# Query columns grouped by dimension, one tile fewer in VectorE's exponential, and paired P·V steps merged, in a four-layer attention kernel

## The chip, the cores and the metric

The kernel runs on one core of a Trainium2 chip. A core has five engines that run their own instruction queues: TensorE (PE) multiplies matrices, and its weight loads are shown apart as PEld; VectorE (DVE) and ScalarE (ACT) work element by element; GpSimd (POOL) does a little side work; SyncE (SP) issues the DMAs. Engines wait for one another on semaphores. Matrix products land in PSUM, everything else lives in SBUF or, for what is set aside, in DRAM.

The metric is the device time of one execution in microseconds (us), the median of the runs shown.

## The reference

The input is a sequence of 2048 tokens with 512 features, in float32. Four layers follow one another, with the weights A, B, A, B. Each layer normalizes, makes 32 query heads of 16 dimensions and one shared key and value head (multi-query attention), takes softmax attention over all 2048 tokens without a mask, and adds the projected result to its input:

```python
def layer(x, wq, wk, wv, wo):          # _A_ref and _B_ref are the same function
    q = (x @ wq).reshape(B, S, H, Dh).transpose(0, 2, 1, 3)   # S 2048, H 32, Dh 16
    k = x @ wk
    v = x @ wv
    scores = jnp.einsum("bhqd,bkd->bhqk", q, k) * (Dh ** -0.5)
    p = jax.nn.softmax(scores, axis=-1)
    o = jnp.einsum("bhqk,bkd->bhqd", p, v)
    return o.transpose(0, 2, 1, 3).reshape(B, S, H * Dh) @ wo

x = A_x
x = x + layer(_layernorm(x), A_wq, A_wk, A_wv, A_wo)
x = x + layer(_layernorm(x), B_wq, B_wk, B_wv, B_wo)
x = x + layer(_layernorm(x), A_wq, A_wk, A_wv, A_wo)
x = x + layer(_layernorm(x), B_wq, B_wk, B_wv, B_wo)
```

The exponentials are the bulk of the elementwise work: 4 layers x 32 heads x 2048 x 2048.

## The kernel before, in words

**Tiling of the attention.** The work is cut into 64 pairs `(l, b, m)`: layer, block of 512 queries, and one of four groups of eight heads. For a pair, the keys come in chunks of 64; one chunk is two halves (`halves`), and a half is a score tile of 128 partitions x 1024 elements. `score()` (letter S of the order) writes one half into a PSUM tile `st` with eight small products that TensorE runs side by side (64 rows by 32 columns each, at eight places of the array), and ScalarE takes its exponential into one of the 16 tiles of `pts` (named `pt` in the trace), line 756. There are two `st` tiles, so TensorE can be one half ahead.

**Exponentials on VectorE.** Of the 4096 halves, 374 do not go to ScalarE. `score_v` puts the scores of such a half, 24 halves ahead of the rest, into the PSUM tile `by_v`, 512 columns at a time; `exp_first` (letter I, line 785) scales them to an integer in the int32 tile `e`; and a chain of six instructions (letters 0 and 1) follows: take the mantissa bits into `mant` (line 800), keep the exponent bits in `e` (line 802), and four multiply-adds that build a polynomial in `pt` and multiply it by `e` (line 794). `e` and `mant` exist twice, so two chains can be open.

**P·V.** `pv(odd)` multiplies 256 queries of two finished halves by the values, in float32, and adds to one of two PSUM tiles `acc`, for the even and the odd rows of the array. The letter `a` does both rows at once. A chunk needs two such steps, `n` = 0 and 1, for queries 0 to 255 and 256 to 511. A float32 product is shown in the trace as two passes, each with a weight load. After the four reads of a chunk (two rows, two `n`) its two `pt` tiles are free again.

**Everything else** (layer norm, the products for K, V, Q and the output, all in split float16 pairs) goes through one PSUM tile `beside`: TensorE's steps of it are the letters N and M inside b to q, VectorE's steps the letter X. Queries of a pair: `q_clamp` (line 420) and `q_rest` (line 427) make a high and a low float16 part `qs` of 128 partitions x 512 queries, partition = head x 16 + dimension, and SyncE stores them to the DRAM scratch `qscr` in four transfers (line 430), one for each half of the heads and each part. Later `load_q` (letter Q, line 724) reads the scratch back with the heads side by side into `qt`. `sq` and `lengths` use the query squares with a small matrix of zeros and ones, `bones`.

**Weights.** For each layer `load_w` brings four chunks of 128 rows of `wq` and `wo` into one of two `wst` buffers, `w_hi` (line 325) makes the high float16 part of a chunk and `w_lo` (line 328) the low part; the load of chunk c + 2 follows `w_lo` of chunk c.

**What sets the order.** Before the main loop a scheduler orders the instructions of the start (the first normalization, the first `wq`, the first queries, K and V). From there on the order of all engines is the string `ORDER` of 14,315 letters, read one by one; each letter emits its instructions in program order on their engines. An engine runs its own queue in order, so a letter decides what stands behind what.

```python
if what == "S":
    score()
elif what in STEPS:
    step(what)
```

Of the kernel before, what the change touches and what calls it, by code (L numbers as in the profile page):

```python
# [201 lines left out]
         "p": "M-", "q": "-M", "r": "V-", "s": "-V"}  # L202


class Work:


# [25 lines left out]
def fast_path(ctx, tc, x_in, weights, out, flag):  # L233
# [79 lines left out]
    def load_w(key, c):  # L313
# [2 lines left out]
        SP.dma_start(t, w[c * P:(c + 1) * P, :])  # L316
        stat[key, c] = t

    def begin_w(key):
        wt[key] = [one.tile([P, NC, D], F16, name=f"{key[0]}{k}") for k in range(2)]  # L320

    def w_hi(key, c):
        if c == 0:
            begin_w(key)
        V.tensor_scalar(wt[key][0][:, c], stat[key, c], WS, None, ALU.mult)

    def w_lo(key, c):
        V.scalar_tensor_tensor(wt[key][1][:, c], stat.pop((key, c)), WS, wt[key][0][:, c],
                               ALU.mult, ALU.subtract)

    def range_w(i, key):
        n = NL * NB + 4 * i + 2 * (key == "wo")
# [92 lines left out]
    def q_rest(l, b, m, ps):  # L425
        qs = stat.pop(("qs", l, b, m))
        V.tensor_tensor(qs[:, 1], ps, qs[:, 0], ALU.subtract)
        for h in range(2):
            for t in range(2):
                SP.dma_start(qscr[l % 2][b][m][h, t].rearrange("d h q -> h d q"),  # L430
                             qs[64 * h:64 * h + 64, t])
        done.add(("q", l, b, m))

    def lengths(l, b, ps):
# [343 lines left out]
    def exp_first():  # L778
        r, new = pend.popleft()
        if new is not None:  # L780
            k = now["e"] = 1 - now["e"]
            assert len(chains) < 2
            fresh.append((one.tile([P, 1024], I32, name=f"e{k}"), k, new))
        e, k, n = fresh[-1]
        V.tensor_scalar(e[:, 512 * r:512 * r + 512], by_v, SCALE / UP / UP * LOG2E * 2.0 ** 23, LEAD,  # L785
                        ALU.mult, ALU.add)
        if new is not None:
            return
        i = tile_of[n]
        p = pts[:, i]  # L790
        mant = one.tile([P, 1024], F32, name=f"mant{k}")

        def write(k, a, c, b):
            n = V.scalar_tensor_tensor(p, a, c, b, ALU.add, ALU.mult).ins  # L794
            if k == 0 and writer[i] is not None:
                tc.declare_no_dep(n, writer[i], reason="behind the reads in between")
            writer[i] = n

        chains.append(deque([
            lambda: V.tensor_scalar(mant.bitcast(I32), e, 0x7FFFFF, 0x3F800000, ALU.bitwise_and,  # L800
                                    ALU.bitwise_or),
            lambda: V.tensor_scalar(e, e, 0x7F800000, None, ALU.bitwise_and),  # L802
            lambda: write(0, mant, C3, mant),
            lambda: write(1, p, C2, mant),
            lambda: write(2, p, C1, mant),
            lambda: write(3, p, C0, e.bitcast(F32))]))

    def chain(k):
        chains[k].popleft()()
        if not chains[k]:  # L810
            chains.pop(k)

    def pv(odd):
        g, c, n = parts[odd].popleft()
        pr, c0, c1 = groups[g]
# [6 lines left out]
        cs = slice(256 * n, 256 * n + 256)  # L822
        x = [pts[:, i[j % 2], (j // 2) * 512 + 256 * n:(j // 2) * 512 + 256 * n + 256]
             for j in range(4)]
        seen.extend(unit)
        read[g, c] = read.get((g, c), 0) + 1
        if read[g, c] == 4:
            ended.extend(unit)
        last = (c, n) == (2 * c1 - 1, 1)
# [6 lines left out]
    def step(what):  # L836
        ops = [[], []]
        for r, w in enumerate(STEPS[what]):
            if w in "EO":
                assert r == "EO".index(w)  # L840
                ops[r].append(pv(r))
            if w in "VW":
                ops[r].append(score_v(r))
            for _ in range({"N": 2, "M": 1, "W": 1}.get(w, 0)):
                ops[r].append(work.next_pe().step(r))
        both(ops)
        for u in seen:
            sees(u)
        seen.clear()
        for u in ended:  # L850
            free.append(tile_of.pop(u))
        ended.clear()
        for g, odd in ends:
            group[odd] += 1
            add_sums(g, odd)
        ends.clear()
# [143 lines left out]

    plan()
    with tc.manual_schedule():
        for what in ORDER:
# [181 lines left out]
```

## Time and profile before

| | |
|---|---|
| median of the runs | 3551.18 us |
| runs | 3549.01, 3551.18, 3562.09 us |
| the profiled execution: time | 3529.43 us |
| its span, first to last instruction | 3527.6 us |
| mean granted TensorE clock | 0.994 |
| busy: PE / DVE / ACT / POOL | 3424.3 / 3288.6 / 3429.4 / 158.8 us |
| exponentials on ScalarE / on VectorE | 3722 / 374 |

The profile is of one execution, which was 21.75 us faster than the median of the timed runs. A group's row gives the engine, the operation, the tiles written and read, the count, then busy time and mean duration, and last the idle time of the engine before these instructions with what ended most of it. Consecutive instructions of an engine overlap at their ends, so a mean duration can be longer than the distance from one start to the next. In a row of the timeline the first two numbers are the start and the duration, both in us, and a bracket gives idle time before it.

### The profile page before, as it was taken

The numbers are of one execution on the slowest core, as the hardware profiler recorded it, in microseconds if no ns is written. First come the engines' busy times: TensorE is split into PE (matmuls) and PEld (weight loads), VectorE is DVE, ScalarE is ACT, GpSimd is POOL, SyncE is SP. The second block draws the span as 40 slices with busy tenths as digits, with TensorE's granted clock in tenths as the row PEclk, the third lists the DMA queues.
The fourth block names the chain that finished last, engine by engine and source line by source line (L and its number), as shares of the span: only waits on it lengthen the run. The fifth ranks groups of instructions, "written<-read, shape, count | busy, mean of one in ns | idle before, by whom it ended". The sixth has DMA issues, their size and how long they took to land.

```text
span 3527.6 us, 234143 instructions
## 1 busy us (share of the span) xinstructions
PE 3424.3 (97%) x111859; PEld 2162.8 (61%) x111859; DVE 3288.6 (93%) x4417; ACT 3429.4 (97%) x3728; POOL 158.8 (5%) x110
## 2 busy tenths in 40 slices
PE   7999999999999999999999999999999999999997
PEld 4666666665666666666566666665656666665653
DVE  4869999999989999999998999999999999999994
ACT  6999999999999999999999999999999999999996
POOL 1000001000000000000000010000000010000000
PEclk9999999999999999999999999999999999999999
DMA  2121111111012111011111111101101111111110
GB/s 93 64 74 45 43 42 33 32 40 46 27 43 63 32 43 48 27 49 36 31 31 60 48 45 50 33 31 39 50 23 37 54 43 35 45 34 40 32 33 20
DMA packets 91837, 149.56 MB, mean 42 GB/s; under 512 B 28985, under 2 KB 45369, under 8 KB 90873
## 3 DMA queue, kind: packets, MB, share of 16 engines
q1 hardware_dynamic: 90872, 134.49, 12.0%
q8 instruction: 876, 14.35, 1.6%
q14 instruction: 89, 0.72, 0.1%
HBM read 90.57 MB, written 34.59 MB: 35 GB/s over the span
## 4 chain that ended last, share of the span: by engine, by line
PE 44%; ACT 43%; DVE 11%; DMA 1%; issue 1%; SPq 0%; POOL 0%; DVEq 0%; ACTq 0%; POOLq 0%
ACT pt L756 43%; PE acc L475 23%; PE st L475 12%; PE beside L475 6%; DVE pt L794 5%; DVE e L785 1%; PE by_v L475 1%; DVE mant L800 1%; DVE e L802 1%; PE beside L372 1%; PE beside L512 1%; DMA rec<-rs 0%; DVE sum L877 0%; SPq L913 0%; DMA qt<-qs 0%
## 5 line engine op out<-in xcount | busy, mean ns | idle before, releaser
L756 ACT ACTIVATE pt<-st 128x1024 f32<-128x1024 f32 x3722 | 3425.2, 1118 | 46.0 <-PE st L475 41.2
L475 PE MATMUL acc<-pt,vop 64*32 64x256 f32 x65536 | 2830.9, 377 | 6.1 <-issue 3.7
L475 PE MATMUL st<-qt,kop 64*32 64x512 f16 x29776 | 1654.3, 381 | 55.1 <-ACT pt L756 36.4
L475 PEld LDWEIGHTS acc<-pt,vop 64*32 64x32 f32 x65536 | 1460.8, 106 | 364.7 <-issue 19.3
L475 PEld LDWEIGHTS <-kop 64*32 64x32 f16 x32768 | 771.3, 90 | 806.2 <-issue 514.8
L794 DVE SCALAR_TENSOR_TENSOR pt<-pt,mant 128x1024 f32<-128x1024 f32 x748 | 913.5, 1221 | 3.7
L785 DVE TENSOR_SCALAR e<-by_v 128x512 int32<-128x512 f32 x748 | 514.0, 687 | 61.2 <-PE by_v L475 33.6
L794 DVE SCALAR_TENSOR_TENSOR pt<-pt,e 128x1024 f32<-128x1024 f32 x374 | 458.6, 1226 | 0.8
L475 PE MATMUL beside<-xnT,wq 64*32 64x512 f16 x5952 | 456.8, 376 | 2.0 <-DVE gv L415 1.1
L794 DVE SCALAR_TENSOR_TENSOR pt<-mant 128x1024 f32<-128x1024 f32 x374 | 455.4, 1218 | 0.0
L475 PE MATMUL beside<-wo,ot 64*32 64x512 f16 x5664 | 432.1, 376 | 4.7 <-issue 2.4
L475 PE MATMUL by_v<-qt,kop 64*32 64x512 f16 x2992 | 298.7, 377 | 2.9 <-DVE e L785 1.5
L802 DVE TENSOR_SCALAR e<-e 128x1024 int32<-128x1024 int32 x374 | 256.7, 686 | 3.2
L800 DVE TENSOR_SCALAR mant<-e 128x1024 int32<-128x1024 int32 x374 | 257.4, 688 | 1.0
L475 PEld LDWEIGHTS <-wq 64*32 64x32 f16 x5952 | 172.4, 92 | 49.3 <-issue 7.9
L475 PEld LDWEIGHTS <-ot 64*32 64x32 f16 x5664 | 163.9, 92 | 49.8 <-issue 10.3
L423 POOL TENSOR_TENSOR sq<-qs 128x512 bf16<-128x512 f16 x64 | 107.9, 1686 | 1066.6 <-DVE qs L420 1066.6
L877 DVE COPY sum<-acc 128x512 f32<-128x512 f32 x128 | 84.4, 682 | 39.4 <-PE acc L475 39.0
L475 PE MATMUL beside<-xnT,wkv 64*32 64x512 f16 x1440 | 107.7, 376 | 0.0
L359 POOL TENSOR_TENSOR rstd<-var,nhalf 128x4 f32<-128x4 f32 x16 | 25.9, 1621 | 1126.5 <-DVE var L358 1126.5
L420 DVE TENSOR_SCALAR qs<-beside 128x512 f16<-128x512 f32 x63 | 43.1, 684 | 25.8 <-PE beside L475 13.3
L448 DVE SCALAR_TENSOR_TENSOR xt<-beside,xt 128x512 f32<-128x512 f32 x64 | 43.8, 684 | 12.3 <-PE beside L512 11.1
(105 smaller groups left out, 755.2 us busy)
## 6 DMA issues: line engine op xcount, KB each, us to landing
qt<-qs SPq DMA_DIRECT2D x85, 512.0 KB
qs<-qs SPq DMA_DIRECT2D x256, 64.0 KB
rec<-rs SPq DMA_DIRECT2D x63, 256.0 KB
xs<-xt SPq DMA_DIRECT2D x48, 256.0 KB
xt<-xs SPq DMA_DIRECT2D x48, 256.0 KB
xt<-in_A_x_dram SPq DMA_DIRECT2D x32, 256.0 KB
sum<-sum SPq DMA_DIRECT2D x252, 32.0 KB
out_dram<-xt SPq DMA_DIRECT2D x16, 256.0 KB
```

Of the source, the lines that this page charges most:

```text
L372: PE.transpose(ps[:, c * P:(c + 1) * P], xn[:, c * P:(c + 1) * P], ident)
L420: V.tensor_scalar(qs[:, 0], ps, BIG, -BIG, ALU.min, ALU.max)
L423: G.tensor_tensor(sq, qs[:, 0], qs[:, 0], ALU.mult)
L448: V.scalar_tensor_tensor(x, ps, 1 / VS / WS, x, ALU.mult, ALU.add)
L475: PE.matmul(o[32 * j:32 * j + 32], w[j][h], x[j][h], start=start, stop=stop, skip_group_check=True, tile_position=(64 * r, 32 * j))
L512: PE.matmul(beside, w, x, start=n == 0, stop=n == 3 * NC - 1)
L756: e = A.activation(pts[:, i], st[s], AF.Exp, scale=SCALE / UP / UP).ins
L785: V.tensor_scalar(e[:, 512 * r:512 * r + 512], by_v, SCALE / UP / UP * LOG2E * 2.0 ** 23, LEAD, ALU.mult, ALU.add)
L794: n = V.scalar_tensor_tensor(p, a, c, b, ALU.add, ALU.mult).ins
L800: lambda: V.tensor_scalar(mant.bitcast(I32), e, 0x7FFFFF, 0x3F800000, ALU.bitwise_and, ALU.bitwise_or),
L802: lambda: V.tensor_scalar(e, e, 0x7F800000, None, ALU.bitwise_and),
L877: V.tensor_copy(sums[pr, odd], acc[odd])
```

## The change

Three things are changed, and `ORDER` stays letter for letter the same.

1. **Query columns by dimension.** `w_hi` and `w_lo` write the columns of `wq` in another order: within 64 columns, dimension by dimension with four heads side by side, where it was head by head. `w_lo` does it in four instructions of 128 columns. The queries then stand in the partitions in the order in which the scratch holds them, and `q_rest` stores both parts of 64 rows with one transfer, two in all, in place of four whose outermost dimension was 4. `bones` follows the new order. What is stored and what `load_q` reads stays the same.
2. **The integer in the exponential's own tile.** `exp_first` writes its integers straight into the `pt` tile of the half; the tile `e` is gone. The polynomial is built in a new tile `poly` (two of them), and only the last multiply-add writes `pt`.
3. **Merged P·V.** When an `a` with `n` = 0 is followed by another `a` with nothing for TensorE between them, both are done in one step of 512 queries; the second letter is skipped. This happens at 201 places: 1608 products of 512 columns take the place of 3216 of 256, of 32,768.

```diff
@@ prologue
-        V.tensor_reduce(bones[:, 0, 0:8], ident.rearrange("p (a b) -> p a b", b=DH), axis=AX.X,
-                        op=ALU.add)
+        V.tensor_reduce(bones[:, 0, 0:8].rearrange("p (r h) -> p r h", h=4),
+                        ident.rearrange("p (r d h) -> p r h d", d=DH, h=4), axis=AX.X, op=ALU.add)
...
+    def by_heads(key, w):
+        return w.rearrange("p (a h d) -> p a h d", h=4, d=DH) if key[0] == "wq" else w
+
+    def by_dims(key, w):
+
+        return w.rearrange("p (a d h) -> p a h d", h=4, d=DH) if key[0] == "wq" else w
...
-        V.tensor_scalar(wt[key][0][:, c], stat[key, c], WS, None, ALU.mult)
+        V.tensor_scalar(by_dims(key, wt[key][0][:, c]), by_heads(key, stat[key, c]), WS, None, ALU.mult)
 
     def w_lo(key, c):
-        V.scalar_tensor_tensor(wt[key][1][:, c], stat.pop((key, c)), WS, wt[key][0][:, c],
-                               ALU.mult, ALU.subtract)
+        t, (hi, lo) = by_heads(key, stat.pop((key, c))), [by_dims(key, w[:, c]) for w in wt[key]]
+        for h in range(4) if key[0] == "wq" else [slice(None)]:
+            n = (slice(None), slice(None), h) if key[0] == "wq" else h
+            V.scalar_tensor_tensor(lo[n], t[n], WS, hi[n], ALU.mult, ALU.subtract)
...
-        for h in range(2):
-            for t in range(2):
-                SP.dma_start(qscr[l % 2][b][m][h, t].rearrange("d h q -> h d q"),
-                             qs[64 * h:64 * h + 64, t])
+        for r in range(2):
+            SP.dma_start(qscr[l % 2][b][m][r].rearrange("t d h q -> (d h) t q"),
+                         qs[64 * r:64 * r + 64])
...
     def exp_first():
         r, new = pend.popleft()
         if new is not None:
-            k = now["e"] = 1 - now["e"]
             assert len(chains) < 2
-            fresh.append((one.tile([P, 1024], I32, name=f"e{k}"), k, new))
-        e, k, n = fresh[-1]
-        V.tensor_scalar(e[:, 512 * r:512 * r + 512], by_v, SCALE / UP / UP * LOG2E * 2.0 ** 23, LEAD,
-                        ALU.mult, ALU.add)
+            fresh.append(new)
+        n = fresh[-1]
+        i = tile_of[n]
+        p = pts[:, i]
+        e = p.bitcast(I32)
+        w = V.tensor_scalar(e[:, 512 * r:512 * r + 512], by_v, SCALE / UP / UP * LOG2E * 2.0 ** 23, LEAD,
+                            ALU.mult, ALU.add).ins
+        if writer[i] is not None:
+            tc.declare_no_dep(w, writer[i], reason="behind the reads in between")
...
+        poly = one.tile([P, 1024], F32, name=f"poly{k}")
+
+        def last():
+            writer[i] = V.scalar_tensor_tensor(p, poly, C0, p, ALU.add, ALU.mult).ins
...
-            lambda: write(0, mant, C3, mant),
-            lambda: write(1, p, C2, mant),
-            lambda: write(2, p, C1, mant),
-            lambda: write(3, p, C0, e.bitcast(F32))]))
+            lambda: V.scalar_tensor_tensor(poly, mant, C3, mant, ALU.add, ALU.mult),
+            lambda: V.scalar_tensor_tensor(poly, poly, C2, mant, ALU.add, ALU.mult),
+            lambda: V.scalar_tensor_tensor(poly, poly, C1, mant, ALU.add, ALU.mult),
+            last]))
...
-    def pv(odd):
+    def pv(odd, whole=False):
+
         g, c, n = parts[odd].popleft()
+        size = 256
+        if whole:
+            assert n == 0 and parts[odd].popleft() == (g, c, 1)
+            size, last_n = 512, 1
...
+    def both_whole(k):
+
+        while k < len(ORDER) and ORDER[k] not in ON_PE:
+            k += 1
+        return (k if k < len(ORDER) and ORDER[k] == "a" and parts[0][0] == parts[1][0]
+                and parts[0][0][2] == 0 else None)
...
             elif what in STEPS:
-                step(what)
+                k = both_whole(k + 1) if what == "a" else None
+                skip.add(k)
+                step(what, k is not None)
```

In the program that results, three places show what is added or moved. The first is TensorE's queue at the first merged step, near the start; `acc_370` and `acc_371` are the two sum tiles before (`acc_380` and `acc_381` now), and each row stands for four products side by side. Before:

```order
L475 MATMUL st_366<-qt,kop_0_102 32x512
L475 MATMUL acc_370<-pt,vop_0_110 32x256 x4
L475 MATMUL acc_371<-pt,vop_0_110 32x256 x4
L475 MATMUL acc_370<-pt,vop_0_110 32x256 x4
L475 MATMUL acc_371<-pt,vop_0_110 32x256 x4
L475 LDWEIGHTS kop_0_102
```

Now:

```order
L486 MATMUL st_376<-qt,kop_0_102 32x512
L486 MATMUL acc_380<-pt,vop_0_110 32x512 x4
L486 MATMUL acc_381<-pt,vop_0_110 32x512 x4
L486 LDWEIGHTS kop_0_102
```

The scores before and after the pair stay where they were; four rows have become two of double width.

The second is SyncE's queue in the start, from the first loads of `wq` (`wst`) to the first load of queries (`qt`); the bracket names the semaphores a transfer waits for (DMAHW: earlier transfers; DVE, PE: engines). Before:

```order
L316 DMA wst<-in_A_wq_dram 128x512 [waits DMAHW6_49,DMAHW2_49,DVE_49]
L345 DMA xt<-in_A_x_dram 128x512 [waits DMAHW3_49,DVE_49]
L345 DMA xt<-in_A_x_dram 128x512 [waits DMAHW4_49,DVE_49]
L345 DMA xt<-in_A_x_dram 128x512 [waits DMAHW5_49,DVE_49]
L316 DMA wst<-in_A_wq_dram 128x512 [waits DMAHW7_49,DVE_49]
L345 DMA xt<-in_A_x_dram 128x512 [waits DVE_49]
L430 DMA qs_0_0_126<-qs 4x16x512 [waits DMAHW0_49,DVE_49]
L430 DMA qs_0_0_126<-qs 4x16x512 [waits DMAHW1_49]
L430 DMA qs_0_0_126<-qs 4x16x512 [waits DMAHW2_49,DVE_49]
L430 DMA qs_0_0_126<-qs 4x16x512 [waits DMAHW3_49]
```

Now:

```order
L357 DMA xt<-in_A_x_dram 128x512 [waits DMAHW2_49,DVE_49]
L357 DMA xt<-in_A_x_dram 128x512 [waits DMAHW3_49,DVE_49]
L357 DMA xt<-in_A_x_dram 128x512 [waits DMAHW4_49,DVE_49]
L319 DMA wst<-in_A_wq_dram 128x512 [waits DMAHW6_49,DMAHW5_49,DVE_49]
L357 DMA xt<-in_A_x_dram 128x512 [waits DVE_49]
L319 DMA wst<-in_A_wq_dram 128x512 [waits DMAHW7_49,DVE_49]
L441 DMA qs_0_0_126<-qs 64x2x512 [waits DMAHW0_49,DVE_49]
L441 DMA qs_0_0_126<-qs 64x2x512 [waits DMAHW1_49]
```

The third chunk of `wq` has moved behind three loads of the next `x`, the fourth behind four, and the four stores are two. On VectorE the scheduler has spread the parts of `w_lo` out: the last part for the first chunk now stands behind the third `xn`, where the second chunk's `w_lo` stood, and the last part for the second chunk behind the four low parts of `xnT`; the loads wait for these.

The third is what waits. ScalarE's queue keeps its 3722 exponentials in order, but 331 of them, those that write a `pt` tile that VectorE used last, now wait for VectorE as well as for TensorE; before, one did. The first one and its neighbours:

```order
L767 ACTIVATE pt<-st_376 128x1024 [waits PE_49]
L767 ACTIVATE pt<-st_377 128x1024 [waits PE_49]
L767 ACTIVATE pt<-st_376 128x1024 [waits DVE_49,PE_49]
L767 ACTIVATE pt<-st_377 128x1024 [waits PE_49]
```

On VectorE the write of `e` waited in 292 of 748 cases for VectorE itself, since its tile was still being read by the chain before; 332 of the 374 instructions that take the mantissa now wait for ScalarE, which wrote the `pt` tile's earlier content. A chain before:

```order
L785 TENSOR_SCALAR e_12975<-by_v 128x512 [waits DVE_49,PE_49]
L785 TENSOR_SCALAR e_12975<-by_v 128x512 [waits PE_49]
L800 TENSOR_SCALAR mant_13146<-e_12975 128x1024 [waits DVE_49]
L802 TENSOR_SCALAR e_12975<-e_12975 128x1024 [waits DVE_49]
L794 SCALAR_TENSOR_TENSOR pt<-mant_13146 128x1024
```

A chain now (rows of other work between them left out in both):

```order
L798 TENSOR_SCALAR pt<-by_v 128x512 [waits PE_49]
L798 TENSOR_SCALAR pt<-by_v 128x512 [waits PE_49]
L812 TENSOR_SCALAR mant_12261<-pt 128x1024 [waits DVE_49,Activation_49]
L814 TENSOR_SCALAR pt<-pt 128x1024 [waits DVE_49]
L815 SCALAR_TENSOR_TENSOR poly_12262<-mant_12261 128x1024
```

The count of VectorE's instructions in a chain stays eight.

More of the change, by code (lines that the diff above doesn't have):

```diff
@@ L780, in exp_first @@
         if new is not None:
-            k = now["e"] = 1 - now["e"]
             assert len(chains) < 2
-            fresh.append((one.tile([P, 1024], I32, name=f"e{k}"), k, new))
-        e, k, n = fresh[-1]
-        V.tensor_scalar(e[:, 512 * r:512 * r + 512], by_v, SCALE / UP / UP * LOG2E * 2.0 ** 23, LEAD,
-                        ALU.mult, ALU.add)
+            fresh.append(new)
[7 more added lines that the diff above has]
+            tc.declare_no_dep(w, writer[i], reason="behind the reads in between")
         if new is not None:
             return
-        i = tile_of[n]
-        p = pts[:, i]
+        k = now["e"] = 1 - now["e"]
         mant = one.tile([P, 1024], F32, name=f"mant{k}")
[L793 to L797, printed above, removed]
+        poly = one.tile([P, 1024], F32, name=f"poly{k}")
+        def last():
+            writer[i] = V.scalar_tensor_tensor(p, poly, C0, p, ALU.add, ALU.mult).ins
         chains.append(deque([
@@ L821, in pv @@
         v = vop[l % 2][c // 8][:, c % 8]
-        cs = slice(256 * n, 256 * n + 256)
-        x = [pts[:, i[j % 2], (j // 2) * 512 + 256 * n:(j // 2) * 512 + 256 * n + 256]
+        cs = slice(256 * n, 256 * n + size)
+        x = [pts[:, i[j % 2], (j // 2) * 512 + 256 * n:(j // 2) * 512 + 256 * n + size]
              for j in range(4)]
         seen.extend(unit)
-        read[g, c] = read.get((g, c), 0) + 1
+        read[g, c] = read.get((g, c), 0) + 1 + whole
         if read[g, c] == 4:
             ended.extend(unit)
-        last = (c, n) == (2 * c1 - 1, 1)
+        last = (c, last_n) == (2 * c1 - 1, 1)
         if last:
@@ L1002, in fast_path @@
     with tc.manual_schedule():
-        for what in ORDER:
+        skip = set()
+        for k, what in enumerate(ORDER):
+            if k in skip:
+                continue
             if what == "S":
```

7 lines of the change are left out of this document (5 added, 2 removed).

## The prediction

> **What bounds the kernel now.** I read the page's busy times and chain first, then ScalarE's row, then ScalarE's timeline for its gaps.
>
> ```profile
> span 3527.6 us, 234143 instructions
> PE 3424.3 (97%) x111859; PEld 2162.8 (61%) x111859; DVE 3288.6 (93%) x4417; ACT 3429.4 (97%) x3728; POOL 158.8 (5%) x110
> PE 44%; ACT 43%; DVE 11%; DMA 1%; issue 1%; SPq 0%; POOL 0%; DVEq 0%; ACTq 0%; POOLq 0%
> L756 ACT ACTIVATE pt<-st 128x1024 f32<-128x1024 f32 x3722 | 3425.2, 1118 | 46.0 <-PE st L475 41.2
> ```
>
> Three engines look full and the chain alternates between two, so shares don't decide. The last row does: the exponentials cover 3425.2 of 3527.6 us, one every 3425.2 / 3722 = 0.920 us, and ScalarE idles only 46.0 us before them. Their number stays 3722. Time can only come from the start, the end, and those 46.0 us; it can be lost wherever ScalarE is made to wait or to run slower. The timeline shows where the idle time sits (start, duration, and in the bracket the gap):
>
> ```profile
> 31.69 1.94 ACT L756 ACTIVATE pt<-st 128x1024 f32<-128x1024 f32 x2 [7.74 <-PE st L475]
> 51.87 125.93 ACT L756 ACTIVATE pt<-st 128x1024 f32<-128x1024 f32 x137 [3.22 <-PE st L475]
> 1896.28 202.79 ACT L756 ACTIVATE pt<-st 128x1024 f32<-128x1024 f32 x221 [4.23 <-PE st L475]
> 2758.64 38.98 ACT L756 ACTIVATE pt<-st 128x1024 f32<-128x1024 f32 x42 [4.85 <-PE st L475]
> 3339.98 155.19 ACT L756 ACTIVATE pt<-st 128x1024 f32<-128x1024 f32 x169 [1.04 <-PE st L475]
> ```
>
> The start takes 31.69 us before the first exponential, the end 3527.6 - 3495.2 = 32.4 after the last. The four large gaps are 20.0 together; they stand where many P·V and product steps are queued ahead of the next score, which the unchanged order keeps. About 26 us remain, in some 40 gaps under 1.4 us.
>
> **Part 1, the start.** This part lies on the path, since nothing runs on ScalarE's exponentials before the first queries are stored and read back. From the timeline and the chain:
>
> ```profile
> 15.21 0.33 SPq L316 DMA_DIRECT2D wst<-in_A_wq_dram  x1
> 15.89 2.47 DVE L380 TENSOR_TENSOR xnT<-tps,xnT 128x512 f16<-128x512 f32 x4
> 18.88 0.42 DVE L325 TENSOR_SCALAR wq<-wst 128x512 f16<-128x512 f32 x1
> 20.99 0.69 DVE L420 TENSOR_SCALAR qs<-qps 128x512 f16<-128x512 f32 x1 [0.96 <-PE qps L974]
> 21.71 2.48 SPq L430 DMA_DIRECT2D qs<-qs  x4
> 21.72 0.69 DVE L427 TENSOR_TENSOR qs<-qps,qs 128x512 f16<-128x512 f32 x1
> ...
> 1.27 2.27 DMA wkvl<-in_A_wk_dram
> 18.42 2.55 PE qps L974 x11
> 23.67 3.48 DMA qs<-qs
> 27.31 3.49 DMA qt<-qs
> 2850.43 3.65 DMA wst<-in_B_wo_dram
> ```
>
> Before, the last chunk of the first `wq` is requested at 15.21 us. Now its transfer waits for the last part of the second chunk's low half, which stands behind the four `xnT` parts. Those end at 18.36; with the parts that now stand ahead of them (three of about 0.2 us) I put them at 18.9 and the request at 19.2. Landing takes between 2.27 (the small `wkvl` load) and 3.65 us (a `wst` load in mid-run): 21.5 to 22.9. Then the high half (0.42) and four low parts (0.8 to 1.3), and about 0.5 for the last two products (2.55 / 11 = 0.23 each): `qs` starts at 23.2 to 25.1 against 20.99, a loss of 2.2 to 4.1; I take 2.8, near the low end, since the queue is nearly empty then.
>
> The stores give some of it back. Before, the second `qs` part ends at 22.41 and the last store lands at 27.15, 4.74 us later. Now both stores wait for the second part, then two issues of 2.48 / 4 = 0.62, so the last begins about 1.15 us after it, and lands 2.27 (the row nearest in size and emptiness) to 3.48 later: 3.4 to 4.6 us, a gain of 0.1 to 1.3. I take 0.9. K's chain follows `qs` on VectorE and has the landing of `qs` and `qt`, 7 us in the rows, to end in. Sum of the start: +1.9 us, bounds +0.9 to +4.0.
>
> **Part 1, later.** The other twelve `wq` chunks (three layers) are made in mid-run; so are 63 of the 64 query stores.
>
> ```profile
> L328 DVE SCALAR_TENSOR_TENSOR wq<-wst,wq 128x512 f16<-128x512 f32 x16 | 10.9, 682 | 0.0
> L325 DVE TENSOR_SCALAR wq<-wst 128x512 f16<-128x512 f32 x16 | 6.7, 418 | 1.7 <-DMA wst<-in_A_wq_dram 1.7
> 10.98 0.26 DVE L298 CAST wkv<-wkvl 128x112 f16<-128x112 f32 x1
> 11.16 0.16 DVE L297 CAST wkv<-wkvl 128x16 f16<-128x16 f32 x1
> 3501.22 0.29 DVE L945 TENSOR_TENSOR sum<-sum,tmp 128x128 f32<-128x128 f32 x1
> ```
>
> A low part of 128 columns is not in the trace. The nearest rows: 112 columns hold VectorE 0.18 us (10.98 to 11.16), a dependent 128-column step takes 0.29 with its end. Four make 0.72 to 1.16, in place of one of 0.60 (0.682 less an overlap of 0.08): +0.12 to +0.56. The high part writes strided columns; it costs +0 to +0.26 (as much as a 0.68 step). I take +0.4 a chunk, 12 x 0.4 = 5 us of VectorE (1.4 to 10). VectorE's idle time hides it (3527.6 - 3288.6 = 239 us); without that cover it would be 5 us. The stores cost 0: of all scores only the first waits for the queries to come back (6.5 us, in the waits shown below), and `sq` reads `qs`, not the transfer.
>
> **Part 2, the integer in `pt`.** The chain has as many instructions of the same shapes, so the busy time stays. What changes is a stall: when the next chain's first `e` follows the last multiply-add of the chain that read the same buffer, it waits for that to finish. The first and the last of 201 such pairs, and a pair without such a wait:
>
> ```profile
> 274.99 1.22 DVE L794 SCALAR_TENSOR_TENSOR pt<-pt,e 128x1024 f32<-128x1024 f32 x1
> 276.32 0.69 DVE L785 TENSOR_SCALAR e<-by_v 128x512 int32<-128x512 f32 x1
> 276.93 1.21 DVE L794 SCALAR_TENSOR_TENSOR pt<-mant 128x1024 f32<-128x1024 f32 x1
> 278.06 0.68 DVE L785 TENSOR_SCALAR e<-by_v 128x512 int32<-128x512 f32 x1
> ...
> 3453.64 1.22 DVE L794 SCALAR_TENSOR_TENSOR pt<-pt,e 128x1024 f32<-128x1024 f32 x1
> 3454.96 0.69 DVE L785 TENSOR_SCALAR e<-by_v 128x512 int32<-128x512 f32 x1
> ```
>
> With the wait `e` starts 0.10 us after its predecessor's end, without it 0.08 before: 201 x 0.18 = 36 us of VectorE, against the 5 it pays for the weights. The Trainium skill's page "VectorE: DVE Perf Modes", section "The DRAIN you can't avoid", says that chaining without semaphores gains nothing, because the pipe empties either way; by that rule this term is 0. The rows above disagree with it.
>
> What VectorE's 31 us are worth is read from TensorE's waits for it (total us, times, longest):
>
> ```profile
> PE beside L475 <- DVE gv L415: 2.9, 4, 1.1
> PE by_v L475 <- DVE e L785: 1.5, 4, 0.5
> PE acc L475 <- DVE sum L877: 1.2, 5, 0.3
> PE st L475 <- DMA qt<-qs: 6.5, 1, 6.5
> ACT pt L756 <- PE st L475: 41.2, 44, 7.7
> ```
>
> The first three are 5.6 us, and not each reaches ScalarE, which has a score in hand. I take 2 us of gain, bounds 0 and 5.6.
>
> The new waits for semaphores are all for work long done when they are met: a `pt` tile is free only after TensorE has read what VectorE or ScalarE had written. They cost at most their own passage, and the nearest row is VectorE's queue, where a second wait is an instruction of its own:
>
> ```profile
> L785 DVEq EVENT_SEMAPHORE  x219: 21/21/21, 276.3 to 3454.9; - x110
> ```
>
> 21 ns each. On ScalarE 331 x 0.021 = 7 us if laid bare; the 1118 ns of the exponential ahead hide it, as the queue runs ahead of the engine. On VectorE 0 likewise, and 219 such waits go. I take 0, upper bound below.
>
> **Part 3, merged P·V.** Two `a` in a row, then the next score:
>
> ```profile
> 1506.75 1.06 PE L475 MATMUL acc<-pt,vop 64*32 64x256 f32 x32
> 1507.61 0.41 PE L475 MATMUL st<-qt,kop 64*32 64x512 f16 x8
> L475 PEld LDWEIGHTS acc<-pt,vop 64*32 64x32 f32 x65536 | 1460.8, 106 | 364.7 <-issue 19.3
> ```
>
> The pair takes 0.86 us (1506.75 to 1507.61). The columns streamed stay the same. Half the weight loads go, 201 x 16 = 3216 of 65,536, but a load of 106 ns runs beside products and is mostly hidden already: gain 0, at most 201 x 0.106 = 21 us of TensorE if every pair shows one, little of it ScalarE's. No score stood between the two, so none comes later. I take 0.
>
> **Sum.** +1.9 start, +0 weights later, -2 VectorE's relief, 0 waits, 0 merge: -0.1 us. On the profiled execution that is 3529.4, against 3529.43; the runs' median lies 21.75 above it, so I forecast 3551 us. From no change a measurement tells about 0.5%, 17.8 us, since the runs shown spread over 13.
>
> **Rivals.**
>
> *ScalarE loses its overlap at the new waits (slower).* The place: the 331 exponentials that reuse one of VectorE's tiles. Exponentials start every 0.920 us and last 1.118, so 0.198 overlap. If the wait keeps the next from entering before the last has ended, it costs 331 x 0.198 = 66 us, straight on the bound: 3617. It decides from 17.8 / 331 = 0.054 us a wait. Against it: the queue's 21 ns. The Trainium skill's "Perfetto Trace Analysis", section "Identifying Dependency Chains", speaks for the mechanism: an instruction that waits for several engines may get a semaphore instruction of its own ahead. "ScalarE: Activation LUTs", section "What ACT_TABLE_LOAD costs", puts the overlap at about 93 ns, from which 331 x 0.093 = 31 us is an estimate, 3582. No run here yet shows it on ScalarE. Chance 0.09.
>
> *Merged steps are dearer than their halves (slower).* If 512 float32 columns ran less evenly, at 0.1 us a step it would cost 201 x 0.1 = 20: 3571; it decides from 0.09. Nothing in the trace speaks for it; the 512-column float16 products keep the rate. Chance 0.05.
>
> *VectorE's relief closes most small gaps (faster).* All 26 us: 3525. For it: VectorE is 93% busy. Against it: TensorE waits for it 5.6 us. It counts as faster from 18 of the 26 on. Chance 0.07.
>
> *The stores and loads bring nothing, the start pays in full.* The start at its upper bound, +4, and no relief: 3555. It falls within the forecast's range.
>
> **How the numbers follow.** No change 0.79 (3551, own range 3541 to 3564: the bounds -5.6 to +4 and the runs' spread), ScalarE's overlap 0.09, merge 0.05, relief 0.07. Faster 0.07, same 0.79, slower 0.14. The range takes in the own range, the milder merge case and half the relief: 3538 to 3572.
>
> **What would show it.** Right: ScalarE's exponentials still 3425 us and 46 idle; the first exponential at 32.6 to 35.7; `pt<-by_v` starting 0.08 before its predecessor's end; merged products twice as long, in pairs of 0.86. Wrong: more ScalarE time or idle time at the 331 waits, merged pairs over 0.95, or TensorE's waits for VectorE growing.

## The result, and the profile after

| | before | this |
|---|---|---|
| median of the runs | 3551.18 us | 3566.71 us |
| range | 3540.89 to 3562.09 us (7 runs) | 3560.57 to 3570.5 us (7 runs) |
| ratio of this to before | | 1.0034, 95% interval 1.0019 to 1.0049 |
| first exponential in the profile | 31.69 us | 34.59 us |

The change makes the kernel slower by 0.34%, about 12 us (7 to 17). The time is inside the range that I gave (3538 to 3572), but outside the 3541 to 3564 of my case of no change, and the sum had come to -0.1 us. The loss is small, under the 0.5% that I had called no change, but the interval leaves zero out. The profiled execution of before was faster than any of its timed runs, so the two profiles differ by 38 us; the experiments below, not that difference, say which part of it counts.

The page of the changed kernel: span and instructions, busy times, the chain's shares, and ScalarE's exponentials with the idle time before them.

```profile
span 3566.0 us, 227922 instructions
PE 3444.0 (97%) x108643; PEld 2122.4 (60%) x108643; DVE 3292.1 (92%) x4465; ACT 3441.3 (97%) x3728; POOL 157.7 (4%) x110
PE 58%; ACT 30%; DVE 9%; issue 2%; DMA 1%; SPq 1%; POOL 0%; DVEq 0%; POOLq 0%
L767 ACT ACTIVATE pt<-st 128x1024 f32<-128x1024 f32 x3722 | 3437.1, 1101 | 70.6 <-PE st L486 65.0
```

ScalarE's idle time before exponentials has risen from 46.0 to 70.6 us, nearly all of it spent waiting for scores. VectorE's average says nothing is wrong: 93% before, 92% now. ScalarE's timeline says where some of the new idle time sits. These are the changed kernel's rows at three places (start, duration, tiles, count, and in the bracket the gap):

```profile
414.42 17.69 ACT L767 ACTIVATE pt<-st 128x1024 f32<-128x1024 f32 x19
432.32 9.27 ACT L767 ACTIVATE pt<-st 128x1024 f32<-128x1024 f32 x10 [0.20 <-PE st L486]
444.17 1.02 ACT L767 ACTIVATE pt<-st 128x1024 f32<-128x1024 f32 x1 [2.58 <-PE st L486]
446.12 1.02 ACT L767 ACTIVATE pt<-st 128x1024 f32<-128x1024 f32 x1 [0.92 <-PE st L486]
447.65 1.02 ACT L767 ACTIVATE pt<-st 128x1024 f32<-128x1024 f32 x1 [0.50 <-PE st L486]
449.17 1.02 ACT L767 ACTIVATE pt<-st 128x1024 f32<-128x1024 f32 x1 [0.50 <-PE st L486]
...
1311.43 19.45 ACT L767 ACTIVATE pt<-st 128x1024 f32<-128x1024 f32 x21 [1.36 <-PE st L486]
...
2164.87 20.50 ACT L767 ACTIVATE pt<-st 128x1024 f32<-128x1024 f32 x22 [2.52 <-PE st L486]
```

At those places VectorE converts the `wq` of the next layer, all four chunks in a burst. What holds ScalarE there can be followed through the engines' timeline of the changed kernel, at the end of the first burst:

```profile
428.35 1.35 DVE L341 SCALAR_TENSOR_TENSOR wq<-wst,wq 128x128 f16<-128x128 f32 x4
...
429.47 0.83 DVE L335 TENSOR_SCALAR wq<-wst 128x512 f16<-128x512 f32 x1
...
439.86 2.32 DVE L345 TENSOR_REDUCE gv<-wq 128x1 f32<-128x2048 f16 x1
442.03 0.27 DVE L351 TENSOR_REDUCE gv<-wkv 128x1 f32<-128x64 f16 x1
442.16 0.74 DVE L459 SCALAR_TENSOR_TENSOR xt<-beside,xt 128x512 f32<-128x512 f32 x1
...
442.95 0.59 PE L523 MATMUL beside<-wo,ot 128*128 128x512 f16 x1 [2.73 <-DVE xt L459]
443.47 0.63 PE L486 MATMUL st<-qt,kop 64*32 64x512 f16 x8
...
444.03 1.46 PE L523 MATMUL beside<-wo,ot 128*128 128x512 f16 x3
444.17 1.02 ACT L767 ACTIVATE pt<-st 128x1024 f32<-128x1024 f32 x1 [2.58 <-PE st L486]
...
445.98 1.04 PE L523 MATMUL beside<-wo,ot 128*128 128x512 f16 x2
```

TensorE's next output product needs the tile `beside`, which VectorE frees with `xt<-beside,xt`; that stands behind the conversions and two reductions in VectorE's queue. TensorE waits 2.73 us, the score behind the product in its queue waits too, and ScalarE has nothing to do. The same place before had this wait already, with 0.35 us in it:

```profile
427.31 2.28 DVE L333 TENSOR_REDUCE gv<-wq 128x1 f32<-128x2048 f16 x1
...
429.63 0.68 DVE L448 SCALAR_TENSOR_TENSOR xt<-beside,xt 128x512 f32<-128x512 f32 x1
...
430.37 0.38 PE L512 MATMUL beside<-wo,ot 128*128 128x512 f16 x1 [0.35 <-DVE xt L448]
...
432.11 0.60 PE L512 MATMUL beside<-wo,ot 128*128 128x512 f16 x2
```

A table by stage shows why. These are windows of before over its first two `wq` bursts and its third (columns: window, length, then busy time of PE, PEld, DVE, ACT and POOL, the granted clock, DMA share and GB/s):

```profile
416.00:432.00 16.00, 14.56 (x440) 8.47 (x424) 15.89 (x23) 16.00 (x18) 0.00 (x0) 1.00 0.25 87
1275.00:1291.00 16.00, 15.16 (x525) 9.38 (x517) 14.17 (x21) 15.07 (x17) 0.00 (x0) 1.00 0.17 53
2120.00:2135.00 15.00, 15.00 (x537) 9.90 (x525) 14.86 (x23) 15.00 (x18) 0.00 (x0) 1.00 0.18 57
```

Of VectorE's 239 us of idle time in the whole span, these three places hold 0.11, 1.83 and 0.14 us. The four chunks of a burst add 4.2 us (worked out below), so there was next to no cover.

### The profile page after: what moved, and what is told of

It is laid out like the page before. It is cut to its first block, busy times and chain, and to the rows that moved or that the text cites. A ratio compares the mean times of both kernels' runs of the same rounds, so it can differ in the third digit from the quotient of the medians.

```text
span 3566.0 us, 227922 instructions
## 1 busy us (share of the span) xinstructions
PE 3444.0 (97%) x108643; PEld 2122.4 (60%) x108643; DVE 3292.1 (92%) x4465; ACT 3441.3 (97%) x3728; POOL 157.7 (4%) x110
## 3 DMA queue, kind: packets, MB, share of 16 engines
q1 hardware_dynamic: 91896, 134.49, 12.9%
HBM read 90.57 MB, written 34.59 MB: 35 GB/s over the span
## 4 chain that ended last, share of the span: by engine, by line
PE 58%; ACT 30%; DVE 9%; issue 2%; DMA 1%; SPq 1%; POOL 0%; DVEq 0%; POOLq 0%
PE acc L486 30%; ACT pt L767 30%; PE st L486 16%; PE beside L486 9%; PE by_v L486 2%; DVE pt L798 1%; DVE pt L809 1%; DVE poly L815 1%; DMA rec<-rs 1%; DVE poly L817 1%; DVE poly L816 1%; DVE mant L812 1%; PE beside L523 1%; PE beside L384 1%; DVE wq L341 0%
## 5 line engine op out<-in xcount | busy, mean ns | idle before, releaser
L767 ACT ACTIVATE pt<-st 128x1024 f32<-128x1024 f32 x3722 | 3437.1, 1101 | 70.6 <-PE st L486 65.0
L486 PE MATMUL acc<-pt,vop 64*32 64x256 f32 (+1 forms) x62320 | 2866.8, 388 | 8.9 <-issue 7.5
L486 PE MATMUL st<-qt,kop 64*32 64x512 f16 x29776 | 1728.6, 381 | 61.1 <-ACT pt L767 37.1
L486 PEld LDWEIGHTS acc<-pt,vop 64*32 64x32 f32 x62320 | 1442.7, 106 | 351.1 <-issue 35.9
L486 PEld LDWEIGHTS <-kop 64*32 64x32 f16 x32768 | 790.1, 90 | 884.1 <-issue 616.6
L798 DVE TENSOR_SCALAR pt<-by_v 128x512 int32<-128x512 f32 x748 | 513.1, 686 | 67.0 <-PE by_v L486 57.4
L809 DVE SCALAR_TENSOR_TENSOR pt<-poly,pt 128x1024 f32<-128x1024 f32 x374 | 459.9, 1230 | 0.8
L817 DVE SCALAR_TENSOR_TENSOR poly<-poly,mant 128x1024 f32<-128x1024 f32 x374 | 458.0, 1225 | 1.5
L816 DVE SCALAR_TENSOR_TENSOR poly<-poly,mant 128x1024 f32<-128x1024 f32 x374 | 456.1, 1220 | 2.2
L815 DVE SCALAR_TENSOR_TENSOR poly<-mant 128x1024 f32<-128x1024 f32 x374 | 455.9, 1219 | 0.0
L812 DVE TENSOR_SCALAR mant<-pt 128x1024 int32<-128x1024 int32 x374 | 257.5, 689 | 2.8
L814 DVE TENSOR_SCALAR pt<-pt 128x1024 int32<-128x1024 int32 x374 | 257.1, 687 | 3.2
```

What stands on the lines that cost most here:

```text
L486: PE.matmul(o[32 * j:32 * j + 32], w[j][h], x[j][h], start=start, stop=stop, skip_group_check=True, tile_position=(64 * r, 32 * j))
L767: e = A.activation(pts[:, i], st[s], AF.Exp, scale=SCALE / UP / UP).ins
L798: w = V.tensor_scalar(e[:, 512 * r:512 * r + 512], by_v, SCALE / UP / UP * LOG2E * 2.0 ** 23, LEAD, ALU.mult, ALU.add).ins
L809: writer[i] = V.scalar_tensor_tensor(p, poly, C0, p, ALU.add, ALU.mult).ins
L815: lambda: V.scalar_tensor_tensor(poly, mant, C3, mant, ALU.add, ALU.mult),
L816: lambda: V.scalar_tensor_tensor(poly, poly, C2, mant, ALU.add, ALU.mult),
```

## The experiments

Each difference below is the ratio to before, measured on the same chip, less one, times 3550 us, with its 95% interval. The ratio is not that of the two medians printed beside it, and the two can differ by 2 to 3 us. Part 1 is the columns by dimension with the two stores, part 2 the integer in `pt`, part 3 the merged steps.

### Each part alone

Part 3 alone is the change's code in `pv`, `both_whole`, `step` and the main loop, nothing else.

> Part 3 alone on the kernel before: 201 pairs of steps merged. Theory A (the loss lies in ScalarE's new waits and in the weights and the start): within 4 us of before, the mean of a merged product near 0.59 us, ScalarE's exponentials and the idle time before them as before (3425 and 46 us in the profile). Theory B (the merged steps make the loss): 8 to 15 us slower, with ScalarE's idle time up by as much. Theory C (TensorE's supply of instructions is what suffers, and 6432 fewer instructions ease it): 0 to 5 us faster, fewer pauses of TensorE inside a step.

Measured: 3549.04 us against 3552.47, ratio 0.9992 (0.9983 to 1.0001), -3 us (-6 to 0). The products of 512 columns cost what the expectation says (merged and unmerged groups of this kernel; the numbers behind the bar are busy time and mean ns):

```profile
L478 PE MATMUL acc<-pt,vop 64*32 64x256 f32 x59104 | 2642.6, 377 | 6.4 <-issue 4.8 <-DVE sum L894 0.8
...
L478 PE MATMUL acc<-pt,vop 64*32 64x512 f32 x3216 | 215.5, 591 | 0.4 <-DVE pt L797 0.4
```

Merging does not make the loss.

Part 2 alone is `exp_first` as in the change, nothing else.

> Part 2 alone: the integer in pt, with its 331 waits of ScalarE for VectorE and VectorE's own stalls gone. Theory A: the waits cost about 32 ns each, 331 x 0.032 = 10.5 us, less VectorE's relief of 0 to 2: 7 to 11 us slower, ScalarE's mean period in unbroken stretches 0.922 us against 0.9195. Theory B (the waits are hidden, the loss lies in part 1): within 3 us of before, period 0.9195. Theory C (relief counts): 2 to 6 us faster.

Measured: 3548.55 against 3552.47, ratio 0.9988 (0.9977 to 0.9999), -4 us (-8 to 0). Theory A (the waits cost time) is out; the value is theory C's, VectorE's relief, but the interval also reaches into theory B's 3 us. The 331 waits on ScalarE are in this kernel too, and it is not slower. The 0.10 us ahead of `by_v`'s step is gone; in the changed kernel the next chain's first step follows a last multiply-add like this:

```profile
283.26 1.22 DVE L809 SCALAR_TENSOR_TENSOR pt<-poly,pt 128x1024 f32<-128x1024 f32 x1
284.39 0.68 DVE L798 TENSOR_SCALAR pt<-by_v 128x512 int32<-128x512 f32 x1
```

It starts 0.09 us before its predecessor's end (283.26 + 1.22 = 284.48), where the waiting ones of before started 0.10 after it.

Part 1 alone:

> Part 1 alone: columns of wq by dimension, with low parts in four instructions, and the queries stored in two transfers. Theory A: the first exponential at 34.6 us against 31.7 (+2.9), and 2 to 8 us of ScalarE's waits near the later wq chunks and after the stores: 5 to 11 us slower. Theory B (hidden, as I forecast): +2 to +4, all of it in the start, ScalarE's idle time after the start as before.

Measured: 3563.94 against 3552.47, ratio 1.0028 (1.0017 to 1.0039), +10 us (6 to 14). Of the three parts only part 1 loses time, and theory B's start cannot make it: see the starts below.

### The waits alone

The kernel before, with one edit: an exponential no longer skips the wait for VectorE when VectorE wrote its tile last.

```diff
-        if writer[i] is not None:
+        if writer[i] is not None and i not in by_chain:
             tc.declare_no_dep(e, writer[i], reason="behind the reads in between")
+        by_chain.discard(i)
...
             writer[i] = n
+            by_chain.add(i)
```

> The kernel before, with nothing but the 331 waits: an exponential that writes a tile which VectorE wrote last also waits for VectorE's last instruction on it, long done by then. Theory A: 32 ns a wait, 7 to 11 us slower, and in the trace a period of 0.922 us against 0.9195. Theory B (the queue's own passage of 17 ns is hidden behind the exponential ahead): within 3 us of before. Should the overlap of 0.198 us be lost at each, it is 66 us.

Measured: 3552.03 against 3552.47, ratio 0.9991 (0.9979 to 1.0003), -3 us (-7 to +1): theory A is out, and the value is at the edge of theory B's 3 us. After the result I had blamed these waits for 10 us, because the profile of the changed kernel shows exponentials 0.9224 us apart in its unbroken stretches where the profile of before has 0.9195. That was a difference between two executions. Merging alone, without one such wait, shows 0.9213 in its profile, and the waits alone 0.9224 in an execution 11 us over that kernel's own median.

### Which half of part 1: conversions or stores

Of part 1 the conversion alone (`by_heads`, `by_dims`, `w_hi`, `w_lo` and `bones` as in the change; `q_rest` as before):

> Of part 1 the conversion alone: the columns of wq by dimension, low parts in four instructions; the queries are stored with the four old transfers, which take the new order for the old one, so that the queries land in wrong places of the scratch and the output is not the reference's. Theory A (the conversions make part 1's loss: about 1 us more of VectorE a chunk, 16 chunks, partly laid bare, and the later loads in the start): 8 to 12 us slower, as part 1 alone was. Theory B (the stores make it): 0 to 3 us slower.

Measured: 3568.69 against 3555.30, ratio 1.0035 (1.0022 to 1.0048), +12 us (8 to 17): theory A.

The stores alone, spread more than the change spreads them:

```diff
-        for h in range(2):
-            for t in range(2):
-                SP.dma_start(qscr[l % 2][b][m][h, t].rearrange("d h q -> h d q"),
-                             qs[64 * h:64 * h + 64, t])
+        for r in range(2):
+            for h in range(4):
+                p = 64 * r + 16 * h
+                SP.dma_start(qscr[l % 2][b][m][r][:, :, h].rearrange("t d q -> d t q"), qs[p:p + 16])
```

> Of part 1 only the spreading of the stores, made eight times as strong: the old column order, each pair's queries stored in eight transfers of 16 rows and both parts (outermost dimension 16) in place of four of 4 x 16 rows. In the start the eight issues (0.62 us each) put the last store about 2.5 us later. Theory A (conversions): that start and nothing else, +1 to +4 us. Theory B (the stores, whose ends now come from 16 DMA engines each and disturb TensorE's supply): 10 us slower or more, with more pauses of TensorE inside a step behind each store.

Measured: 3567.81 against 3555.30, ratio 1.0035 (1.0021 to 1.0050), +12 us (7 to 18): theory B's number, not theory A's +1 to +4. Its profile has the first exponential at 34.28, 0.5 after its peers. TensorE's pauses that the profile puts to issue, that is, to nothing it shows, are 17.1 us, little over the 12.6 to 16.5 of the kernels with parts 2 and 3 (each and both), so theory B's mechanism is not shown. Eight transfers a pair do cost something in mid-run, and what it is stays open. It does not explain the change: there are two transfers a pair in it, and part 1 with them (+10) is no slower than the conversion with the four old ones (+12).

### Time in the burst, or the strided columns

Every `wq` conversion done twice, in plain columns:

```diff
-        V.tensor_scalar(wt[key][0][:, c], stat[key, c], WS, None, ALU.mult)
+        for _ in range(2 if key[0] == "wq" else 1):
+            V.tensor_scalar(wt[key][0][:, c], stat[key, c], WS, None, ALU.mult)
...
+        for _ in range(2 if key[0] == "wq" else 1):
+            V.scalar_tensor_tensor(wt[key][1][:, c], t, WS, wt[key][0][:, c], ALU.mult, ALU.subtract)
```

> The kernel before with every wq conversion done twice, to the same place: 0.418 + 0.682 = 1.10 us more of VectorE a chunk, in plain unbroken columns, about what the new conversion adds (1.05). Nothing else is changed. Theory A (VectorE's time in the bursts of four chunks is laid bare one to one): 12 later chunks x 1.1 = 13, 8 to 14 us slower, with TensorE's waits beside <- xt up from 8 to 14 us or more. Theory B (the strided columns or the four small steps do the harm, not the time): within 4 us of before. My forecast's step (VectorE's idle time hides it) also says within 4.

Measured: 3565.41 against 3544.40, ratio 1.0065 (1.0045 to 1.0085), +23 us (16 to 30). Theory A's mechanism, and more than its number: in this kernel the start pays too (first exponential at 41.25 us, since its loads also wait for the doubled steps). TensorE's waits for `xt<-beside,xt` (total us, times, longest), in before's two rows, and in this kernel's:

```profile
PE beside L512 <- DVE xt L448: 7.7, 4, 5.8
...
PE beside L475 <- DVE xt L448: 0.4, 1, 0.4
```

```profile
PE beside L514 <- DVE xt L450: 11.2, 4, 5.8
PE beside L477 <- DVE xt L450: 7.8, 2, 4.1
```

8.1 us have become 19.0, and 7.4 of the 8.1 stand at the end of the kernel, outside the bursts. In the changed kernel they are 14.3:

```profile
PE beside L523 <- DVE xt L459: 10.7, 4, 6.4
...
PE beside L486 <- DVE xt L459: 3.6, 2, 2.2
```

The same time on VectorE, but not in the bursts: the mantissa of every twentieth chain taken twice.

```diff
+        def mantissa():
+            for _ in range(2 if twice else 1):        # twice: every twentieth chain
+                V.tensor_scalar(mant.bitcast(I32), e, 0x7FFFFF, 0x3F800000, ALU.bitwise_and, ALU.bitwise_or)
```

> The kernel before with the mantissa of every twentieth chain on VectorE taken twice: 18 x 0.69 = 12.4 us more of VectorE, as much as the new conversions add in mid-run, but one piece at a time, some 190 us apart. Theory A (what costs is time in the bursts, where VectorE has no idle time; elsewhere its idle time does hide a piece): within 5 us of before. Theory C (VectorE bounds the kernel throughout, so any time on it is laid bare): 9 to 14 us slower.

Measured: 3552.55 against 3548.14, ratio 1.0007 (0.9998 to 1.0015), +2 us (-1 to +5): theory A. VectorE does the extra 18 instructions (392 in place of 374):

```profile
L805 DVE TENSOR_SCALAR mant<-e x392: 628/687/972, 104.6 to 3490.1; 128x1024 int32<-128x1024 int32 x196
```

So 12 us of VectorE cost about 2 where they are spread, and 12 to 13 us cost 9 to 18 where they fall into the three bursts.

The exponentials come in the same order in all kernels, so the bursts can be priced one by one: how much more time than in before passes from ten exponentials ahead of the burst to twenty behind its start, worked out from each profile's ScalarE timeline (us):

| kernel | layer 2's `wq` | layer 3's | layer 4's | sum |
|---|---|---|---|---|
| merge alone | 1.6 | -0.6 | 0.1 | 1.1 |
| integer in `pt` alone | 1.4 | -0.8 | -0.1 | 0.5 |
| waits alone | 1.6 | 0.7 | -0.1 | 2.2 |
| stores in eight | 0.6 | -0.4 | 0.0 | 0.2 |
| mantissa twice | 0.3 | 0.3 | 0.0 | 0.6 |
| part 1 alone | 5.6 | 1.8 | 2.7 | 10.1 |
| conversion alone | 5.2 | 3.2 | 4.5 | 12.9 |
| the change | 5.5 | 0.9 | 3.0 | 9.4 |
| conversion twice, plain | 6.5 | 5.6 | 5.8 | 17.9 |

The second burst, which had 1.83 us of idle VectorE in the window, is the cheapest of the three in every kernel with dearer conversions. But in before ScalarE itself was idle for 0.93 us in that window (15.07 of 16.00 us busy), which makes the differences there look smaller.

The waits are only part of these prices. Without those at the end of the kernel, TensorE waits for `xt<-beside,xt` 0.7 us in before, 6.3 in the change, 7.6 in part 1 alone, 7.6 in the conversion alone and 11.7 with the conversion twice. Much of the rest goes with a lower TensorE clock behind the waits. These are two windows of the changed kernel after the first burst (the granted clock is the third number from the end):

```profile
443.00:446.00 3.00, 3.00 (x21) 0.55 (x21) 3.00 (x4) 1.02 (x1) 0.00 (x0) 0.50 0.23 87
446.00:449.00 3.00, 3.00 (x36) 0.69 (x36) 2.10 (x3) 2.05 (x2) 0.00 (x0) 0.50 0.00 0
```

In the trace's record of the clock this half clock lasts 6.8 us at the first burst of the four kernels with dearer conversions, 3.4 us in merge, `pt` and waits alone (the 1.4 to 1.6 us of their first column), and is not there in before, with the stores in eight and with the mantissa twice. Over the three bursts it lasts 6.8 us in the change and in part 1 alone, 13.7 in the conversion alone and 17.1 with the conversion twice. If half of that time is lost (an estimate from the granted clock of 0.50), added waits and clock make 9.0, 10.3, 13.7 and 19.5 us, against the sums 9.4, 10.1, 12.9 and 17.9 of the table. What sets the clock back is not shown: the changed kernel's waits of 1.4 and 2.2 us in the other two bursts left it at 1.00, and after the same wait of 0.4 us at the first burst merge alone had the half clock and the mantissa twice had not.

### Off VectorE, and without part 1

High parts of the later `wq` chunks on GpSimd, in the changed kernel:

```diff
-        V.tensor_scalar(by_dims(key, wt[key][0][:, c]), by_heads(key, stat[key, c]), WS, None, ALU.mult)
+        E = V if key[0] == "wo" or key[1] == 0 else G
+        E.tensor_scalar(by_dims(key, wt[key][0][:, c]), by_heads(key, stat[key, c]), WS, None, ALU.mult)
```

> The changed kernel with the high parts of the twelve later wq chunks on GpSimd, so 12 x 0.79 = 9.5 us less of VectorE, in the bursts. Theory A: 5 to 10 us faster than the changed kernel, so +2 to +8 against before, if GpSimd's step is short enough (under 2 us) to be done when the low part wants it; a step of 3 us or more would keep the burst as long, and nothing would be gained. Theory B (not VectorE's time): as the changed kernel, +12 to +15.

Measured: 3551.68 against 3544.40, ratio 1.0020 (1.0008 to 1.0033), +7 us (3 to 12). That is in theory A's range, but the mechanism is not seen: the first burst still costs 6.0 us, TensorE's waits for `xt<-beside,xt` in mid-run are 6.2 us against the change's 6.3, and the interval overlaps that of the change. GpSimd's step is long enough to be waited for:

```profile
L336 POOL TENSOR_SCALAR wq<-wst x12: 2223/2479/3209, 416.3 to 2151.7; 128x512 f16<-128x512 f32 x12
```

2.48 us in the median, against 0.79 on VectorE.

Parts 2 and 3 without part 1:

> Parts 2 and 3 without part 1. Each alone came out 0.1% under before, at the edge of what the runs tell. If they add up: 4 to 10 us faster than before. If those were chance: within 3 us. If they hinder each other (more of TensorE's supply stalls): slower than before by 2 or more.

Measured: 3550.33 against 3555.30, ratio 0.9985 (0.9973 to 0.9997), -5 us (-10 to -1). That agrees with their adding up, and this version is 0.15% faster than before, where the change was 0.34% slower. The same with the later high parts on GpSimd:

> Parts 2 and 3 without part 1 (that was 5 us under before), and the high parts of all later weight chunks, wq and wo, on GpSimd: 28 x 0.42 = 12 us less of VectorE. Theory A: 3 to 10 us faster than parts 2 and 3 alone, so 8 to 15 under before, if GpSimd's step is under 2 us. If GpSimd is slow, the low parts wait for it and it comes out 0 to 10 us slower than parts 2 and 3 alone.

Measured: 3539.95 against 3544.40, ratio 0.9987 (0.9976 to 0.9999), -5 us (-9 to 0). GpSimd brings nothing more, where I had expected 3 to 10 us. The bursts of parts 2 and 3 alone have no gap for it to close; this is ScalarE's timeline of that kernel over the first and the second:

```profile
409.50 31.38 ACT L759 ACTIVATE pt<-st 128x1024 f32<-128x1024 f32 x34
...
1272.70 60.68 ACT L759 ACTIVATE pt<-st 128x1024 f32<-128x1024 f32 x65 [0.24 <-PE st L478]
```

## Why the prediction was wrong, point by point

**The weights in mid-run: the step that failed.** I wrote "VectorE's idle time hides it (3527.6 - 3288.6 = 239 us); without that cover it would be 5 us." Both halves were wrong. The cover is an average over the span, and the place had next to none: 0.11 us in the first burst's window. TensorE's waits, from which I quoted other rows, have one of `beside` for `xt` of 0.4 us in mid-run (the 7.7 us of the larger row are nearly all at the end), which names the place; one table by windows would have told it. None of my rivals stood at this place either. And the size: I took +0.4 us a chunk. These are the groups of the changed kernel, with low parts of 128 columns and the high part:

```profile
L341 DVE SCALAR_TENSOR_TENSOR wq<-wst,wq 128x128 f16<-128x128 f32 x64 | 21.8, 506 | 0.1
...
L335 DVE TENSOR_SCALAR wq<-wst 128x512 f16<-128x512 f32 x16 | 12.7, 793 | 0.7 <-DMA wst<-in_A_wq_dram 0.7
```

Four low parts hold VectorE 21.8 / 16 = 1.36 us where one held it 10.9 / 16 = 0.68, and the high part 0.79 where it was 0.42: +1.05 us a chunk, 12.6 for twelve, beyond my upper bound of 10. The 128-column row that I leaned on (0.29 us each) is on plain columns; these are 0.34 apart. The strided high part was bounded by "as much as a 0.68 step" and costs 0.79. The three bursts then lose 9 to 13 us in the profiles with the conversion, where I had put the term at 0: TensorE waits there for the `beside` tile, ScalarE for TensorE's scores, and part of the loss goes with the half clock behind the waits.

**The start.** Forecast +1.9 (32.6 to 35.7), measured 34.59 in the changed kernel and 34.03 with part 1 alone. But 31.69 was not the usual start of before: the kernels whose start is unchanged (merge, `pt`, waits, and the two parts together) have 33.69 to 33.83, since their eleven query products ran at 0.35 to 0.40 us each, not 0.23. The row of before is in the prediction; this is parts 2 and 3 together:

```profile
18.39 4.34 PE L992 MATMUL qps<-xnT,wq 128*128 128x512 f16 x11
```

Against those the start lost 0.2 to 0.9 us. The parts of the sum are there: `qs` starts at 25.28 against 20.99 (22.76 in parts 2 and 3 together), and from the end of the second `qs` part to the last landing pass 3.2 us where it was 4.7, so that the two stores give back 1.5, not 0.9. The conversion alone, with the four old stores, has its first exponential at 36.68, 2.7 after part 1 with two:

```profile
36.68 1.94 ACT L765 ACTIVATE pt<-st 128x1024 f32<-128x1024 f32 x2 [9.90 <-PE st L484]
```

**VectorE's relief.** Right as far as the runs tell: -2 forecast (0 to -5.6), -4 measured (-8 to 0), out of the 36 us that I worked out for VectorE. It is the other side of the same coin: time taken off VectorE all over the span is worth little, since it is spread. The rows stand as I read them: a first step starts 0.10 us after its predecessor's end with the wait, and 0.09 before it without. The Trainium skill's "VectorE: DVE Perf Modes", section "The DRAIN you can't avoid", says that chaining without semaphores doesn't skip the emptying of the pipe, by which the term would be 0; these rows disagree. The same section of the Trainium skill says that a next operation that is not held starts earlier, and with that they agree.

**The waits.** Right: 0, and the 66 us of the lost overlap did not come. The waits alone are -3 us (-7 to +1).

**The merge.** Right as far as the runs tell: 0 forecast, -3 us (-6 to 0), with the product at 0.591 us for 512 columns.

**The stores later.** 0 forecast; nothing in the runs speaks against it for two transfers, though why eight cost 12 us is open.

Part 1 at +10 and parts 2 and 3 at -5 add to +5, and the change measures +12 (7 to 17). With the intervals of all three this gap of 7 us has an uncertainty of about 8, so whether the parts hinder each other stays open.

## What to carry to other kernels

Idle time hides work only where it is: before calling added work hidden, take the engine's busy time in a window around the place where it lands, and look for whoever already waits a little (0.35 us here) for the instruction behind it. Some 12 us of an engine that is 93% busy cost 9 or more in three bursts and 2 when spread. And a single profile of a kernel whose runs spread by 20 us can show a slower pace, later starts and more stalls that belong to the execution and not to the change; each part alone, timed, tells them apart.

## What the runs showed of the hardware that I had not expected

- Writing float16 with a stride of four columns made VectorE's 512-column scaling 793 ns in place of 418.
- A semaphore instruction of its own (17 ns) ahead of 331 exponentials cost nothing that can be measured, -3 us (-7 to +1), though ScalarE is 97% busy.
- After the 2.73 us that TensorE waited in the first burst, its products came at little over half the pace: `beside<-wo,ot` took 1.04 us for two, where before they took 0.60 (rows at 445.98 and 432.11 above), and the granted clock was 0.50 from 443 to 449 us.
- The same eleven products of the start ran at 0.23 us each in some executions and 0.35 to 0.40 in others, 2 us of difference in the first exponential; why is open.
- Eight query stores a pair in place of four cost about 12 us over the run, with no single wait in the profile that accounts for it.
